# A spectral mixing and gated convolution kernel: blocks in time order, a paired 32x32 convolution, batch 0 turned on chip, single PSUM banks, products shared with GpSimd

## The chip, the cores and the metric

The kernel runs on one core of a Trainium2 chip. Five engines work side by side, each through its own list in order: TensorE (PE, with its weight loads shown as PEld), VectorE (DVE), ScalarE (ACT), GpSimd (POOL) and SyncE (SP, which here only issues DMAs). The time is that of one execution on the device, in microseconds (us). Lower is better.

## What is computed

The input x has 8 batches of 3200 points in time and 256 channels. Along time it is filtered in the frequency domain with one complex filter per channel. The result y then passes a gated unit: a causal convolution of five taps per channel gives the gate, and a gated projection is projected once more.

```python
X = np.fft.rfft(x, axis=1)
Y = X * (filt_r + 1j * filt_i)[None]
y = np.fft.irfft(Y, n=3200, axis=1)
for k in range(5):                       # yp is y with 4 zeros ahead
    gate_pre += conv_w[k][None, None, :] * yp[:, k:k + 3200, :]
gate = 1 / (1 + np.exp(-gate_pre))
out = (gate * (y @ w_val)) @ w_out
```

## The kernel before

Time is written as t = 32 a + r, with a from 0 to 99 (L = 100) and the residue r from 0 to 31 (R = 32). A transform over a, one over r, a product with the filter, and the two inverse transforms make the mixing. In order, for each batch:

- `load_x` (issued by POOL, L161) brings four residues (RC = 4) of all a, converted to bf16, into a tile xt; eight loads a batch, ten buffers.
- `s1` (L417) multiplies by the table cf_t, and `so` copies the result from PSUM to the tile so, of which there is one. `turn` (L436) transposes in 32x32 blocks on DVE into tt, four instructions a batch.
- `s2` (L446) multiplies by w_t in seven units (UCH: six of two frequencies per group and one of one). `xs` copies the unit out of PSUM, `zed` (L464) makes the two products with the real and the imaginary filter on DVE, `inva` (L477) transforms back, `ue` copies to u. The copies `so`, `xs`, `ue` and `oe` are made by one helper, on ACT (L408) or on DVE (L410).
- `wr` (L498, issued by SP) writes u to a DRAM buffer escr, and `lv` (L508, L509) reads it back in another arrangement into vt, four residues at a time in two DMAs, with four buffers. This round trip moves the index from partitions to rows.
- `ib` (L518) multiplies by the table ci_t, `ye` (L528) copies to y on ACT, in the order residue by residue; `halo` (L535, L537) copies the four residues that the causal convolution needs, on POOL.
- For each of eight chunks of four residues, 400 points: `conv` (L545) with 64x64 diagonal matrices, `gate` (L554, sigmoid on ACT), `val` (L563), `gv` (L573, the gate times the value, on DVE), `outp` (L583), `oe`, and `store` in two DMAs (L597, L598).

PSUM is used through four buffers of two banks each (`psum()`). Ahead of the first batch tables are computed, the filters are loaded by POOL in 32 DMAs (L222, L225, L228) and copied to a second group of partitions by SP (L253). Weights come by POOL (`load_w`).

The order on each engine is written by a planner, the class `Plan`: every step is a task with an engine, a booked cost, a rank, its predecessors and the buffers it takes and gives back. The planner runs through the tasks in its own time and picks at each moment the ready task with the lowest rank. What comes out is a fixed list per engine; on the chip an engine works through it in order and waits where a step is not ready. For `s1` the ranks are 8 b + j, and the other stages follow with offsets.

Of the kernel before, what the change touches and what calls it, by code (L numbers as in the profile page):

```python
# [15 lines left out]
PI = math.pi  # L16
L = 100
# [5 lines left out]
NCH = R // RC  # L23
UCH = [(m, min(2, NM - m)) for m in range(0, NM, 2)]
ICH = [NCH - 1] + list(range(NCH - 1))
MAGIC = 12582912.0


class Plan:
# [3 lines left out]
    def __init__(self, room, stay=1.0):  # L33
        self.tasks, self.room, self.stay = {}, dict(room), stay

    def add(self, name, engines, rank, deps, emit, take=(), give=(), land=0.0, mode=None):
        self.tasks[name] = dict(engines=engines, rank=rank, deps=deps, emit=emit, take=take,
                                give=give, land=land, mode=mode)

    def run(self):  # L40
# [6 lines left out]
        ready_at = {n: 0.0 for n in left}  # L47
        free = {}
        mode = None
        gives = []  # L50
        ready = {n for n in left if need[n] == 0}
        order = []
        now = 0.0
        while left:
            gives.sort()
            while gives and gives[0][0] <= now + 1e-9:
                for pool in gives.pop(0)[1]:
                    self.room[pool] += 1
            best = None
            for n in ready:  # L60
                t = left[n]
                if ready_at[n] > now + 1e-9:
                    continue
                if any(self.room[p] < 1 for p in t["take"]):
                    continue
                for e, cost in t["engines"].items():
                    if free.get(e, 0.0) <= now + 1e-9:
                        away = e == "PE" and t["mode"] != mode
                        key = (t["rank"] + (self.stay if away else 0.0), cost)
                        if best is None or key < best[0]:  # L70
                            best = (key, n, e, cost)
            if best is None:
                later = [ready_at[n] for n in ready if ready_at[n] > now + 1e-9]
                later += [v for v in free.values() if v > now + 1e-9]
                later += [g[0] for g in gives if g[0] > now + 1e-9]
                assert later, ("stuck", sorted(ready)[:20], self.room)
                now = min(later)
# [4 lines left out]
            for p in t["take"]:  # L82
                self.room[p] -= 1
            if e == "PE":
# [5 lines left out]
            if t["give"]:  # L90
                gives.append((end + 0.1, t["give"]))
            for u in users.get(n, ()):
                need[u] -= 1
                ready_at[u] = max(ready_at[u], end + 0.1 + t["land"])
                if need[u] == 0:
                    ready.add(u)
            order.append((t["emit"], e))
        self.span = max(free.values())
        return order


@with_exitstack
def kernel(
# [10 lines left out]

# [15 lines left out]
    DQ = D // E  # L130

    cpool = ctx.enter_context(tc.tile_pool(name="const", bufs=1))
    cf_t = cpool.tile([128, 2, 2, 32], FP16, name="cf_t")
    ci_t = cpool.tile([128, L], FP16, name="ci_t")
# [3 lines left out]
    fr_t = cpool.tile([128, 2, NM, D], BF16, name="fr_t")  # L138
    fi_t = cpool.tile([128, 2, NM, D], BF16, name="fi_t")
    dg_t = cpool.tile([128, 2, K, 64], BF16, name="dg_t")  # L140
    wv_t = cpool.tile([128, 2, D], BF16, name="wv_t")
    wo_t = cpool.tile([128, 2, D], BF16, name="wo_t")

    pp = ctx.enter_context(tc.tile_pool(name="ps", bufs=4, space=bass.MemoryType.PSUM))
    dpool = ctx.enter_context(tc.tile_pool(name="scr", bufs=2, space=bass.MemoryType.DRAM))
    NXT = 10
    xpool = ctx.enter_context(tc.tile_pool(name="xin", bufs=NXT))
    sopool = ctx.enter_context(tc.tile_pool(name="s1o", bufs=1))
    tpool = ctx.enter_context(tc.tile_pool(name="s2i", bufs=2))
    zpool = ctx.enter_context(tc.tile_pool(name="zed", bufs=3))  # L150
    upool = ctx.enter_context(tc.tile_pool(name="ivo", bufs=4))

    def psum():
        return pp.tile([128, 1024], FP32, name="ps", tag="ps")

    st = {}

    def load_x(b, j):
        xt = xpool.tile([128, RC, D], BF16, name="xt")
        src = x[b].rearrange("(a r) d -> a r d", r=R)[:, RC * j:RC * j + RC, :]  # L160
        nc.gpsimd.dma_start(out=xt[0:L], in_=src)  # L161
        st["X", b, j] = xt

    g1 = ctx.enter_context(tc.tile_pool(name="gen", bufs=1))
# [10 lines left out]
    V = nc.vector  # L175

# [3 lines left out]
    def frac(t, n, shape):  # L180
        y = g1.tile(shape, FP32, name=f"fy{n}")
        V.tensor_scalar(y[...], t[...], MAGIC, MAGIC, op0=ALU.add, op1=ALU.subtract)
        V.tensor_tensor(y[...], t[...], y[...], op=ALU.subtract)
# [5 lines left out]
    g = {}  # L189

    def fsrc(f, row, ap):
        return bass.AP(tensor=f.tensor, offset=f.offset + row * D, ap=ap)

    FCUT = [(0, 6), (6, NM)]

    def pool_setup():
# [3 lines left out]
        for j in range(3):  # L200
            load_x(0, j)
# [5 lines left out]
        for j in range(3, NCH):  # L207
            load_x(0, j)
# [6 lines left out]
        for m0, m1 in FCUT:  # L215
            nm = m1 - m0
            for f, dst in ((filt_r, fr_t), (filt_i, fi_t)):
                for t in range(2):
                    p = 64 * t
                    k = NM * t + m0  # L220
                    for h in range(2):
                        nc.gpsimd.dma_start(  # L222
                            out=dst[p:p + 16, h, m0:m1, :].rearrange("p m d -> p (m d)"),
                            in_=fsrc(f, k + NS * h, [[100 * D, 16], [1, nm * D]]))
                    nc.gpsimd.dma_start(  # L225
                        out=dst[p + 16:p + 32, 0, m0:m1, :],
                        in_=fsrc(f, 100 - k, [[100 * D, 16], [-D, nm], [1, D]]))
                    nc.gpsimd.dma_start(  # L228
                        out=dst[p + 16:p + 32, 1, m0:m1, :],
                        in_=fsrc(f, 100 - k - NS, [[100 * D, 16], [-D, nm], [1, D]]))  # L230

    def load_w():
        for dh in range(2):
            for r in range(2):
                ch = 128 * dh + 64 * r
                nc.gpsimd.dma_start(
                    out=wv_t[:, dh, :].rearrange("p (r h j) -> p h r j", r=2, h=2)[:, r],
                    in_=moe_w_val[128 * dh:128 * dh + 128, 128 * r:128 * r + 128]
                    .rearrange("p (h j) -> p h j", h=2))
                nc.gpsimd.dma_start(out=wo_t[64 * dh:64 * dh + 64, r, :],  # L240
                                    in_=moe_w_out[ch:ch + 64, :])

    def sp_setup():
        cw = g["cw"] = g1.tile([128, 2, K], FP32, name="cw")
        for dh in range(2):
            nc.sync.dma_start(
                out=cw[:, dh, :],
                in_=moe_conv_w[:, 128 * dh:128 * dh + 128].rearrange("k d -> d k"))
        for m0, m1 in FCUT:
            for dst in (fr_t, fi_t):  # L250
                for t in range(2):
                    p = 64 * t
                    nc.sync.dma_start(out=dst[p + 32:p + 64, :, m0:m1, :],  # L253
                                      in_=dst[p:p + 32, :, m0:m1, :])

    def cf_dve():
# [10 lines left out]
    def cf_act():  # L267
# [3 lines left out]
    def w_dve():  # L271
        pcol = g["pcol"]
        ge = []
        for i, v in enumerate((31.5, 63.5, 95.5)):
# [26 lines left out]
        room = (ypool.tile([128, 2, H + R, L], BF16, name="yt")[...]  # L301
                .rearrange("p h r a -> p (h r a)").bitcast(FP32))
        t, y = (room[:, NS * 64 * n:NS * 64 * n + NS * 64].rearrange("p (s k) -> p s k", k=64)
# [8 lines left out]
    def w_act():  # L312
# [3 lines left out]
    def eye():  # L316
# [9 lines left out]
    TCH = [(0, 4), (4, 8), (8, 12), (12, NM)]  # L326

    def tab_pe(i):
        m0, m1 = TCH[i]
        ps = psum()  # L330
        for m in range(m0, m1):
            for h, t in ((0, 0), (1, 1), (0, 1), (1, 0)):
                rows = slice(64 * h, 64 * h + 64)
                o = 512 * h + 128 * (m - m0)
                nc.tensor.matmul(ps[64 * t:64 * t + 64, o:o + 128],
# [3 lines left out]
        st["tab", i] = ps  # L339

    def tab_ev(i, w, e):
        m0, m1 = TCH[i]
        src = st["tab", i][:, :].rearrange("p (h m b k) -> p h m b k", h=2, b=2, k=64)
# [9 lines left out]
    def ci_dve():  # L353
        vi, vh, vc, vt = col("vi"), col("vh"), col("vc"), col("vt")
        ii = g1.tile([128, 1], I32, name="ii")
        ts(ii[...], g["pcol"][...], 1.0, ALU.mult)
        ij = [g1.tile([128, 1], I32, name=f"ij{n}") for n in range(5)]
        ts(ij[0][...], ii[...], 3, ALU.logical_shift_right)
        ts(ij[4][...], ii[...], 2, ALU.logical_shift_right)
        ts(ij[1][...], ii[...], 1, ALU.logical_shift_right)  # L360
        ts(ij[2][...], ii[...], 1, ALU.bitwise_and)
        ts(ij[3][...], ij[1][...], 1, ALU.bitwise_and)
        ts(ij[1][...], ij[4][...], 1, ALU.bitwise_and)
        for o, n in ((vi, 0), (vt, 1), (vc, 2), (vh, 3)):
# [376 lines left out]
```

## Time and profile before

| What | Value |
|---|---|
| median of 3 runs | 345.65 us (344.83 to 347.17) |
| span of the profiled execution | 344.8 us |
| granted TensorE clock, mean | 0.970 of full |
| instructions in the profile | 9785 |
| hardware DMA queue (SP): packets, MB | 45344, 55.20 |
| software DMA queue (POOL): packets, MB | 12032, 15.08 |

The profile holds one execution. An engine's busy time is the union of its instructions; a matmul's row includes the time that it takes to pass through the array, so a busy PE is not a PE at its peak. A group's row gives line, engine, operation, tiles and shape, the count, then the busy time and the mean of one in ns, then the idle time of the engine ahead of the group and what ended it. In the chain that ended last each piece is followed by what it released; a row has its start, its length and what it is. A row of the stretches has the stretch, its length, the busy time and the instructions of PE, PEld, DVE, ACT and POOL, the granted clock, the mean busy share of the 16 DMA engines and GB/s. The share of the DMA engines counts packets that wait too, and can pass 1.

### The profile page before, as it was taken

What the parts mean: (1) busy time and instruction counts of PE and PEld (TensorE: products, weight loads), DVE (VectorE), ACT (ScalarE), POOL (GpSimd) and SP (SyncE); (2) the same over time, 40 slices, a digit from 0 to 9 for tenths busy, and PEclk for the clock granted to TensorE, in tenths of its full rate; (3) what the DMA queues carried; (4) which work ended last, traced back from release to release, by engine and by line L of the source; (5) the groups of instructions that cost most, each with busy time, mean ns of one, the idle gap of its engine ahead of it and who ended that gap; (6) DMA issues with size and microseconds to landing.
All of it is one profiled execution on the core that took longest, in us unless ns stands there. A gap on an engine that the chain in (4) does not pass through costs nothing.

```text
span 344.8 us, 9785 instructions
## 1 busy us (share of the span) xinstructions
PE 288.3 (84%) x3988; PEld 191.6 (56%) x3988; DVE 256.4 (74%) x340; ACT 267.8 (78%) x309; POOL 68.0 (20%) x142
## 2 busy tenths in 40 slices
PE   2634677639999987999779997999999999999992
PEld 0023031326667755776457764776577677766762
DVE  4985477938698996889849994989798999734541
ACT  3954286928898987898849986998999789887663
POOL 8687455210112112110211011100100000001000
PEclk9999999969999999899989998999999999999997
DMA  6999999995899989898869969795677568778544
GB/s 95 155 168 163 213 192 195 206 238 168 199 232 247 272 233 231 245 229 251 170 200 207 271 176 250 214 245 171 199 208 221 156 204 261 234 214 248 160 144 143
DMA packets 57421, 70.91 MB, mean 206 GB/s; under 512 B 8608, under 2 KB 37152, under 8 KB 57376
## 3 DMA queue, kind: packets, MB, share of 16 engines
q1 hardware_dynamic: 45344, 55.20, 53.4%
q0 software_dynamic: 12032, 15.08, 29.0%
q8 instruction: 31, 0.51, 0.6%
q14 instruction: 14, 0.11, 0.1%
HBM read 43.78 MB, written 39.85 MB: 243 GB/s over the span
## 4 chain that ended last, share of the span: by engine, by line
PE 43%; DMA 24%; DVE 15%; ACT 7%; issue 4%; POOL 4%; SPq 1%; ACTq 0%; POOLq 0%; DVEq 0%
DMA vt<-escr 13%; PE ps L583 12%; PE ps L545 10%; DMA xt<-in_x_dram 6%; PE ps L563 6%; DVE tt L436 5%; DVE gv L573 5%; PE ps L417 5%; PE ps L518 5%; PE ps L477 4%; DMA fi_t<-in_filt_i_dram 3%; PE ps L446 3%; ACT o L408 2%; DVE xs L410 2%; POOL xt L161 2%
## 5 line engine op out<-in xcount | busy, mean ns | idle before, releaser
L573 DVE TENSOR_TENSOR gv<-ps,gt 128x800 bf16<-128x800 f32 x64 | 62.7, 980 | 19.9 <-PE ps L563 13.6
L408 ACT ACTIVATE o<-ps 100x1024 f32<-100x1024 f32 x59 | 61.0, 1035 | 16.9 <-PE ps L583 12.9
L410 DVE CAST xs<-ps 128x1024 bf16<-128x1024 f32 (+1 forms) x44 | 50.4, 1145 | 29.0 <-PE ps L446 29.0
L583 PE MATMUL ps<-wo_t,gv 128*100 128x256 bf16 x512 | 68.7, 278 | 2.7 <-DVE gv L573 1.1
L545 PE MATMUL ps<-yt,dg_t 64*64 64x400 bf16 x1280 | 67.3, 339 | 0.3
L408 ACT ACTIVATE so<-ps 128x1024 bf16<-128x1024 f32 x53 | 54.5, 1029 | 15.9 <-PE ps L417 11.1
L528 ACT ACTIVATE yt<-ps 128x800 bf16<-128x800 f32 x64 | 53.9, 846 | 15.9 <-PE ps L518 15.7
L583 PEld LDWEIGHTS <-gv 128*100 128x100 bf16 x512 | 54.5, 125 | 18.6 <-DVE gv L573 9.0
L161 POOL DMA_DIRECT2D xt<-in_x_dram x64 | 35.4, 556 | 124.5 <-PE ps L417 119.8
L554 ACT ACTIVATE gt<-ps 128x800 bf16<-128x800 f32 x64 | 54.1, 847 | 6.5 <-PE ps L545 5.3
L417 PE MATMUL ps<-xt,cf_t 100*128 100x512 bf16 x128 | 47.5, 462 | 12.2 <-DMA xt<-in_x_dram 11.2
L563 PE MATMUL ps<-yt,wv_t 128*128 128x400 bf16 x256 | 54.4, 335 | 0.5 <-ACT gt L554 0.5
L408 ACT ACTIVATE u<-ps 128x1024 bf16<-128x1024 f32 (+1 forms) x46 | 44.9, 982 | 7.2 <-PE ps L477 6.6
L518 PE MATMUL ps<-ci_t,vt 104*128 104x100 f16 x512 | 34.3, 212 | 16.5 <-DMA vt<-escr 16.4
L518 PEld LDWEIGHTS <-vt 104*128 104x128 bf16 x512 | 29.6, 100 | 30.1 <-DMA vt<-escr 19.8
L545 PEld LDWEIGHTS <-dg_t 64*64 64x64 bf16 x1280 | 34.5, 108 | 17.3 <-issue 4.2
L436 DVE STREAM_TRANSPOSE tt<-so 128x1024 f32<-128x1024 f32 x32 | 40.6, 1272 | 3.2 <-ACT so L408 3.2
L464 DVE TENSOR_TENSOR za<-xs,fr_t 128x1024 bf16<-128x1024 bf16 (+1 forms) x56 | 36.1, 649 | 1.4 <-ACT xs L408 0.2
L464 DVE TENSOR_TENSOR zb<-xs,fi_t 128x1024 bf16<-128x1024 bf16 (+1 forms) x56 | 35.5, 640 | 1.4 <-DMA fi_t<-in_filt_i_dram 1.4
L477 PE MATMUL ps<-zb,b_t 64*64 64x256 bf16 x416 | 29.7, 294 | 4.4 <-DVE zb L464 4.4
L477 PE MATMUL ps<-za,a_t 64*64 64x256 bf16 x416 | 30.3, 298 | 2.4 <-DVE za L464 2.1
L446 PE MATMUL ps<-tt,w_t 64*64 64x256 bf16 x416 | 24.2, 305 | 9.0 <-DVE tt L436 4.4
(93 smaller groups left out, 181.9 us busy)
## 6 DMA issues: line engine op xcount, KB each, us to landing
out_dram<-o SPq DMA_DIRECT2D x64, 384.0 KB
xt<-in_x_dram POOLq DMA_DIRECT2D x64, 200.0 KB, 6.7
escr<-u SPq DMA_DIRECT2D x48, 256.0 KB
vt<-escr SPq DMA_DIRECT2D x64, 192.0 KB
escr<-u SPq DMA_DIRECT2D x8, 128.0 KB
vt<-escr SPq DMA_DIRECT2D x64, 16.0 KB
out_dram<-o SPq DMA_DIRECT2D x64, 16.0 KB
fr_t<-in_filt_r_dram POOLq DMA_DIRECT2D x8, 56.0 KB, 4.7
```

Of the source, the lines that this page charges most:

```text
L408: nc.scalar.activation(dst, src, AF.Copy, **kw)
L410: nc.vector.tensor_copy(dst, src)
L417: nc.tensor.matmul(ps[:, 512 * h:512 * h + 512], lhsT=cf_t[0:L].rearrange("p h c i -> p (h c i)"), rhs=xv[:, DQ // 2 * h:DQ // 2 * h + DQ ...
L436: nc.vector.transpose(dst, src)
L464: (nc.vector if e == "DVE" else nc.gpsimd).tensor_tensor(z[:, :, 0:nm * D], xs_[:, :, 0:nm * D], f[:, :, m0:m0 + nm, :].rearrange("p h m d ...
L477: nc.tensor.matmul(ps[64 * h:64 * h + 64, 512 * t + D * a:512 * t + D * a + D], lhsT=tab[rows, h, m0 + a, :], rhs=zz[w][rows, h, D * a:D * ...
L518: nc.tensor.matmul(ps[:, o:o + L], lhsT=v[0:NV, a, 128 * dh:128 * dh + 128], rhs=ci_t[0:NV, :], start=True, stop=True)
L545: nc.tensor.matmul(ps[64 * dh:64 * dh + 64, 512 * r:512 * r + RC * L], lhsT=dg_t[rows, dh, k, :], rhs=y[rows, dh, RC * j + k:RC * j + k + ...
L554: nc.scalar.activation(g[...], ps[:, :].rearrange("p (h n) -> p h n", h=2)[:, :, 0:RC * L], AF.Sigmoid)
L563: nc.tensor.matmul(ps[:, 512 * eh:512 * eh + RC * L], lhsT=wv_t[:, dh, 128 * eh:128 * eh + 128], rhs=y[:, dh, H + RC * j:H + RC * j + RC, ...
L573: nc.vector.tensor_tensor(gv_[...], ps[:, :].rearrange("p (h n) -> p h n", h=2)[:, :, 0:RC * L], g[...], op=ALU.mult)
L583: nc.tensor.matmul(ps[0:L, D * a:D * a + D], lhsT=gv_[:, eh, L * a:L * a + L], rhs=wo_t[:, eh, :], start=(eh == 0), stop=(eh == 1))
```

## The change

The kernel is rewritten around the same mathematics.

- y is stored in time order: `ye` writes runs of four points. The halo copy is gone. The gated unit works on blocks of 512 points, six and one of 128 (`BLOCKS`). `conv` takes two blocks at a time (`PAIRS`), with sixteen 32x32 tiles in place of four 64x64 ones; it depends on all `ye` of its batch. `outp` reads every fourth point of a block as its stationary operand, 128 rows at a time instead of 100, and `store` writes four rows of 1 KB per partition in one DMA.
- Batch 0 doesn't go through DRAM: `ue` writes to a tile of its own layout, and `turn2`, four DVE transposes, makes vt out of it; `ib` and `ye` of batch 0 run per half of the channels, with a second column of the table ci_t.
- PSUM is one tile of eight banks. The planner hands out single banks; `val`, `gv`, `outp` and `oe` work on one bank each, in halves.
- In batches 1 to 7 the products of units 0, 2, 3, 5 and 6 are made by GpSimd (`pool_u`), those of 1 and 4 by DVE. The list books 0.15 + 1.05 nm us for one of them, 2.25 us for a full unit (nm = 2).
- x is loaded by eight residues (XR = 8), four loads a batch, six buffers. `turn` works in place, in two so tiles. vt is one tile of a whole batch, with one DMA for four residues. The filters come in 24 DMAs. `ci_dve` moves from DVE to POOL, `diag` from DVE to ACT.
- The planner has a model of the DMA queues and of the banks, and each stage and batch has a rank of its own, written in a table (`CFG`).

```diff
+XR = 8
+NXC = R // XR
-ICH = [NCH - 1] + list(range(NCH - 1))
+BLK = 512
+BLOCKS = [(i * BLK, BLK) for i in range(6)] + [(6 * BLK, 128)]
+PAIRS = [(0, 1), (2, 3), (4, 5), (6,)]
+CFG = dict(
+    turned=(0,),
+    pool_u=((), (0, 2, 3, 5, 6)),
+    room=dict(xt=6, so=2, xs=3, z=4, u=4, e=2, v=8, y=2, g=4, gv=4, o=3),
...
+            if u in cfg["pool_u"][min(b, 1)]:
+                for w in range(2):
+                    add(f"z{b},{u},{w}", {"POOL": 0.15 + 1.05 * nm}, "z", b, u,
...
+                add(f"z{b},{u}", {"DVE": 0.06 + 0.545 * nm}, "z", b, u, [f"xs{b},{u}"] + fl,
...
+            for q in range(4):
+                add(f"t2{b},{q}", {"DVE": 1.16}, "t2", b, q, [f"ue{b},{u}" for u in range(NU)]
...
+            add(f"cv{b},{p}", {"PE": 1.12 if len(js) == 2 else 0.35}, "cv", b, js[0], yes + ["dg"],
+                ("conv", b, p), banks=2 * len(js), take=("g",) * len(js), mode=2)
...
+    PS = pp.tile([128, NB, 512], FP32, name="ps")
+    VT = vpool.tile([128, R, D], BF16, name="vt")
...
+    def load_x(e, b, c):
+        xt = xpool.tile([128, XR, D], BF16, name="xt")
+        src = x[b].rearrange("(a r) d -> a r d", r=R)[:, XR * c:XR * c + XR, :]
         nc.gpsimd.dma_start(out=xt[0:L], in_=src)
...
+    def turn(e, b, q):
+        v = words(st["SO", b], q)
+        nc.vector.transpose(v, v)
...
+    def turn2(e, b, q):
+        w = D // 8
+        ut = st["UT", b][...].bitcast(FP32)
+        src = bass.AP(tensor=ut.tensor, offset=ut.offset + NS * w * q,
+                      ap=[list(ut.ap[0]), [2 * NS, DQ // 4], [1, 2], [2, 32]])
+        dst = (VT[...].rearrange("p r d -> p (r d)").bitcast(FP32)
+               .rearrange("p (r n) -> p n r", r=R)[:, w * q:w * q + w]
+               .rearrange("p (q w) r -> p q w r", w=2))
+        nc.vector.transpose(dst, src)
...
-        nc.sync.dma_start(out=v[0:96], in_=sv[0:96])
-        nc.sync.dma_start(out=v[96:NV], in_=sv[96:NV])
+        nc.sync.dma_start(out=VT[0:NV, RC * i:RC * i + RC, :], in_=sv)
...
+        y = st["Y", b][:, hs[0]:hs[-1] + 1, H:]
+        nc.scalar.activation(
+            y.rearrange("p h (a r) -> p h a r", r=R)[:, :, :, RC * i:RC * i + RC],
+            st.pop(("ib", b, i, hs))[:, :, 0:RC * L].rearrange("p h (r a) -> p h a r", r=RC),
+            AF.Copy, scale=1.0 / N)
+
+    def conv(e, b, p, bk):
+        y = st["Y", b]
+        js = PAIRS[p]
+        tiles = [(i, j) for s in range(4) for i in range(4) for j in [(i + s) % 4]]
+        for k in range(K):
+            for i, j in tiles:
+                ih, half = divmod(i, 2)
+                dh, x = j & 1, ih ^ (j >> 1)
+                if x >= len(js):
+                    continue
+                n0, n = BLOCKS[js[x]]
+                rows = slice(32 * i, 32 * i + 32)
+                nc.tensor.matmul(PS[32 * j:32 * j + 32, bk[2 * x + half], 0:n],
+                                 lhsT=dg_t[rows, dh, k, :], rhs=y[rows, dh, n0 + k:n0 + k + n],
+                                 start=(k == 0), stop=(k == K - 1))
...
+            for a in range(2):
+                for r in range(2):
+                    nc.tensor.matmul(PS[:, bk[0], D * a:D * a + D],
+                                     lhsT=gv_[:, r, 2 * h + a:n:4], rhs=wo_t[:, j & 1, r, :],
+                                     start=(r == 0), stop=(r == 1))
...
+            nc.sync.dma_start(out=out[b, n0:n0 + n].rearrange("(p i) d -> p (i d)", i=4),
+                              in_=o[...].rearrange("p h n -> p (h n)"))
```

More of the change, by code (lines that the diff above doesn't have):

```diff
@@ L89, in run @@
             free[e] = end
[L90 to L97, printed above, removed]
+            self.start[n] = (now, end, e)
+            freed = [] if t["free"] is None else [held[k][i] for k, ii in t["free"] for i in ii]
```

892 lines of the change are left out of this document (503 added, 389 removed), and 33 rows, old and new, of the table move.

## The prediction

> **What bounds the kernel now.** I read the page's busy line and its slices, then stretches by stage, then the chain that ended last, then the groups kept apart by shape.
>
> ```profile
> span 344.8 us, 9785 instructions
> ...
> PE 288.3 (84%) x3988; PEld 191.6 (56%) x3988; DVE 256.4 (74%) x340; ACT 267.8 (78%) x309; POOL 68.0 (20%) x142
> ...
> PE   2634677639999987999779997999999999999992
> ...
> DVE  4985477938698996889849994989798999734541
> ACT  3954286928898987898849986998999789887663
> ...
> DMA  6999999995899989898869969795677568778544
> ...
> DMA packets 57421, 70.91 MB, mean 206 GB/s; under 512 B 8608, under 2 KB 37152, under 8 KB 57376
> ...
> PE 43%; DMA 24%; DVE 15%; ACT 7%; issue 4%; POOL 4%; SPq 1%; ACTq 0%; POOLq 0%; DVEq 0%
> ```
>
> No engine is the bound alone. Three are near full in the middle (the digits 8 and 9), GpSimd is idle for 80% of the span, and the first nine slices (78 us) are thin on PE, DVE and ACT while the DMA row is full. So there are two stories: a slow start, and a middle in which three engines and the DMA hand work to each other. The chain shows both.
>
> ```profile
> 26.16 5.19 DMA fi_t<-in_filt_i_dram
> 34.36 11.60 DMA xt<-in_x_dram
> ...
> 63.07 11.63 DMA vt<-escr
> 74.75 0.85 PE ps L518 x8
> ...
> 154.53 1.25 DVE tt L436
> ...
> 193.72 1.25 DVE tt L436
> ...
> 231.22 1.25 DVE tt L436
> ...
> 265.55 1.25 DVE tt L436
> ...
> 302.11 0.97 PE ps L545 x20
> 303.08 1.01 PE ps L583 x8
> 304.08 0.68 PE ps L563 x4
> ```
>
> The turn (L436) recurs once a batch: 39.2, 37.5 and 34.3 us apart. At the start the chain goes filters, the next batch's input, the read back of batch 0 from DRAM. I cut the span at the convolution (L545) of the first and of the last batch.
>
> ```profile
> 79.12 1.89 PE L545 MATMUL ps<-yt,dg_t 64*64 64x400 bf16 x40
> ...
> 315.01 2.09 PE L545 MATMUL ps<-yt,dg_t 64*64 64x400 bf16 x40
> ```
>
> That gives 79.1 us of start, 235.9 us for seven batch steps (33.7 each), and 29.8 us from 315.0 to 344.8.
>
> **The evacuations, the turn and the products (DVE and ACT).** These are the groups that change.
>
> ```profile
> L408 ACT ACTIVATE o<-ps 100x1024 f32<-100x1024 f32 x59 | 61.0, 1035 | 16.9 <-PE ps L583 12.9 <-ACT yt L528 1.5 <-DMA vt<-escr 1.4
> ...
> L528 ACT ACTIVATE yt<-ps 128x800 bf16<-128x800 f32 x64 | 53.9, 846 | 15.9 <-PE ps L518 15.7
> ...
> L408 ACT ACTIVATE u<-ps 128x1024 bf16<-128x1024 f32 x40 | 41.4, 1040 | 5.8 <-PE ps L477 5.1 <-ACT xs L408 0.4 <-DMA vt<-escr 0.2
> L436 DVE STREAM_TRANSPOSE tt<-so 128x1024 f32<-128x1024 f32 x32 | 40.6, 1272 | 3.2 <-ACT so L408 3.2
> L161 POOL DMA_DIRECT2D xt<-in_x_dram x64 | 35.4, 556 | 124.5 <-PE ps L417 119.8 <-DMA xt<-in_x_dram 2.1 <-DMA fi_t<-in_filt_i_dram 0.9
> ...
> L464 DVE TENSOR_TENSOR za<-xs,fr_t 128x1024 bf16<-128x1024 bf16 x48 | 32.8, 689 | 1.2
> L464 DVE TENSOR_TENSOR zb<-xs,fi_t 128x1024 bf16<-128x1024 bf16 x48 | 32.5, 682 | 1.4 <-DMA fi_t<-in_filt_i_dram 1.4
> ...
> L410 DVE COPY o<-ps 100x1024 f32<-100x1024 f32 x5 | 6.1, 1222 | 4.7 <-PE ps L583 3.4 <-DMA vt<-escr 1.4
> ...
> L408 ACT ACTIVATE u<-ps 128x512 bf16<-128x512 f32 x6 | 3.6, 593 | 1.5 <-PE ps L477 1.5
> ...
> L464 DVE TENSOR_TENSOR za<-xs,fr_t 128x512 bf16<-128x512 bf16 x8 | 3.2, 405 | 0.2 <-ACT xs L408 0.2
> L464 DVE TENSOR_TENSOR zb<-xs,fi_t 128x512 bf16<-128x512 bf16 x8 | 3.1, 390 | 0.0
> ```
>
> Products: in batches 1 to 7, four full units and the half unit go to GpSimd, 4 x (0.689 + 0.682) + 0.405 + 0.390 = 6.28 us a batch, 44.0 us off DVE. Output copies: 64 of 1024 columns become per batch twelve of 512 and one of 256, 6400 columns for 8192, so 0.22 x (61.0 + 6.1) = 14.7 us go; there are 104 of them, 40 more, and the u rows put the fixed part of one at 2 x 593 - 1040 = 146 ns, so 5.8 us come back. The gated products (L573) become 104 for 64 in the same way, 5.8 us more; the gates fall from 64 to 56, 1.2 us less. Batch 0 adds four turns, 5.1 us, and eight more y copies, 1.2 us. Sum: -44.0 - 14.7 + 5.8 + 5.8 - 1.2 + 5.1 + 1.2 = -42.0 of 524.2 us (256.4 + 267.8), 8%. The lists balance the two engines, so I apply it to both: 30.1 us a batch each for 32.8.
>
> The y copy writes runs of four points and reads PSUM with a stride of 100. No row has that. I take 0, since the equal 1024-column copies above cost the same whatever they write (1035 and 1040). The upper end is a doubling, 0.85 x 8 = 6.8 us a batch on ACT; a lower price than contiguous has no reason.
>
> **PE.** By the chain, twenty convolution matmuls take 0.97 us, eight output ones 1.01, four value ones 0.68. Output falls from 64 to 50 matmuls a batch: 14 x 0.126 = 1.8 us less. Its stationary operand is now read with a stride of four; I take 0, and the other end is that the loads stop hiding behind the matmuls, one more 0.126 for each of the 50, 6.3 us. The convolution does five taps with sixteen 32x32 tiles at a time on 512 points each, a pair of blocks at once. If sixteen tiles overlap as the four 64x64 tiles do, a pair costs 0.97 x 512/400 = 1.24 us and the last 128 points at most 0.97 x 128/400 = 0.31: 4.0 us a batch for 7.8. If only four overlap, it costs 16 us. I take the first, because x20 in 0.97 us (49 ns each, for 400 columns) already shows tiles running together. [...] PE loses 5.6 us a batch of 36.0 (288.3 / 8), value and the other stages being the same columns. New here: a convolution waits for all eight y copies of its batch, not for two. Behind it in PE's order stand the value and output matmuls; the cover is the next batch's first stages, placed between, and two y buffers.
>
> **GpSimd, and what waits behind it.** A product there has no row; the halo copies are nearest.
>
> ```profile
> L537 POOL COPY yt<-yt x16: 511/515/653, 76.5 to 313.1; 128x396 bf16<-128x396 bf16 x16
> ```
>
> ```profile
> 283.21 0.68 DVE L464 TENSOR_TENSOR zb<-xs,fi_t 128x1024 bf16<-128x1024 bf16 x1
> ...
> 283.61 1.11 POOL L537 COPY yt<-yt 128x396 bf16<-128x396 bf16 x2 [27.73 <-ACT yt L528]
> ```
>
> One input of 396 elements takes 0.515 us, 1.3 ns each; a product of 1024 is between 1.33 us (the second input free) and 2.66 (each input read for itself). The new list books 2.25, which I use: 8 x 2.25 + 2 x 1.2 = 20.4 us a batch, and four loads of 0.556 make 22.6, under a 30 us step at either end. The input loads now stand in POOL's queue behind products, up to 4.5 us late; six buffers of a quarter batch each cover that.
>
> The longest copy, 0.653 us, is in the pair that starts at 283.61, inside a DVE product that ends at 283.89. It is the only sign of a collision: up to 0.14 us for 0.28 us of overlap. The other way round, a DVE product behind a GpSimd product, no row shows. Four products a batch stay on DVE, between those of GpSimd; each may wait from 0 to 2.25 us, 0 to 9 us a batch. I take 0.5 each, 2 us, between the row and the ends. [...]
>
> **The start.** SP's queue is part of it.
>
> ```profile
> 34.22 28.63 SPq L498 DMA_DIRECT2D escr<-u  x8
> ```
>
> Reading batch 0 back could not begin before 63.07, because SP's order puts a write of batch 1 ahead, and it lasted 11.63 us. Both go. In their place come four turns (5.1 us) and y copies (8 x 0.846 + 1.2 = 8.0 us, beginning after two turns). The filters set the earliest point: the last lands at 31.35; they now take 24 issues for 32, some 4 us less of POOL's queue at 0.556, so 27, and 4 us for the copy to the other partitions, then 3 us for the last unit: 34. Then 2.5 + 8 = 44.5, and batch 1's first stage uses the same engines: 50 us, with 44 and 60 as ends (60: the input of batch 1 again blocks PE, as the 11.60 us piece does). Constants moved to GpSimd and ACT lie inside these 50 us; I cost them at nothing, and if GpSimd is late with the table of L518, the y copies wait.
>
> **The steps.** Stores and reads back are one DMA each instead of two, so SP has about half the issues; SP was not the bound.
>
> ```profile
> 0.00:50.00 50.00, 26.39 (x220) 10.10 (x221) 33.28 (x85) 28.38 (x33) 33.64 (x72) 1.00 0.97 162
> ...
> 110.00:260.00 150.00, 137.05 (x1995) 96.60 (x1994) 124.74 (x144) 128.57 (x150) 17.86 (x37) 0.97 0.85 222
> ```
>
> From 110 to 260 us PE is busy 91%, ACT 86%, DVE 83%. A step of 33.7 less 8% is 31.0. The waits for DRAM on the chain in the steps (5 to 7 us a batch where they stand) shrink, since a whole batch of read-back slots stands free instead of half and single PSUM banks let copies free space sooner: I take 2.5 us off, and add the 2 us of collisions: 30.5. The end loses PE work, 1.8 + 3.8 = 5.6 us: 24.2.
>
> Sum: 50 + 7 x 30.5 + 24.2 = 287.7 us of span, against 344.8. The median of the runs, 345.65, is 0.9 above that span, so 289 us by the clock of the runs.
>
> **Rivals.** (1) DVE waits for GpSimd at half a product each time, 1.13 x 4 = 4.5 us a batch instead of 2: 33 us a step, 306. For it: the one overlap above; against: DVE has slack of 17%. (2) The DMA binds. Batch 0's trip (104 x 32 x 256 x 2 bytes each way, 3.4 MB) goes, 67.5 MB stay; 8.1 MB move in the first 50 us, so 59.4 MB in 238 us is 250 GB/s, where 110 to 260 shows 222 at a share of 0.85. If 222 is the limit, the rest takes 268 us: 319. Against: 0.85 is not full; 222 / 0.85 = 261. (3) The tiles overlap less than said: eight at once make the convolution cost 8 us a batch as now, PE keeps 36.0 - 1.8 = 34.2 us a step and becomes the bound, and the end is 28: 318. (4) Faster still: the lists are packed without gaps. Then copies overlap at their ends, as these two do.
>
> ```profile
> 202.59 1.02 ACT L408 ACTIVATE so<-ps 128x1024 bf16<-128x1024 f32 x1 [0.78 <-ACT gt L554]
> 203.51 1.02 ACT L408 ACTIVATE o<-ps 100x1024 f32<-100x1024 f32 x1
> ```
>
> They start 0.92 us apart and last 1.02, so 30.1 us of copies fit into 27 to 28; with a start of 45 and steps of 27.5 that is 263. Against: PE has 30 us of its own by the same kind of sum.
>
> (5) Slower: GpSimd becomes the bound. It has 9 product sizes and 2.2 us of loads a batch; to lose, a step must reach 38.6 us ((345.65 - 0.9 - 50 - 24.2) / 7), so a product must take (38.6 - 2.2) / 9 = 4.0 us. At twice the booked time, 4.5 us, a step is 42.7 and the kernel 374. Against: the rows' upper end is 2.66, and DVE holding it off adds at most 0.69.
>
> **Chances.** Forecast 0.57 (its own range 274 to 304), rivals in order 0.14, 0.09, 0.05, 0.09, 0.06. A measurement here tells about 1% from no change. Faster by more: the forecast and rivals 1 to 4, 0.94, of which I give 0.02 to within 1%, where two of them come together; slower: 0.06. Leaving out rival 5, the upper half of 2 and the lower part of 4 gives 266 to 317.
>
> **What would show it.** The first convolution near 50 us; turns some 30 us apart; L545's successor at 1.2 to 1.6 us a pair; GpSimd busy for 20 to 24 us a batch, with no idle ended by PE; DVE products still near 0.68. DVE products over 1.5 us show rival 1; a DMA row of nines with engines waiting for vt, rival 2; pairs over 2.4 us, rival 3; products of 4 us on GpSimd, rival 5. I am wrong if the first convolution is after 60 us or the steps exceed 34.

## The result and the profile after

The changed kernel takes 464.95 us (median of four runs, 459.59 to 471.43) where the kernel before took 345.72 beside it: 1.336 times as long, 95% interval 1.327 to 1.346. Ratios leave out executions in a slower state of the chip, such as the 471.43 here, while medians count all. The forecast was 289. From here on line numbers are those of the changed kernel (`so`, `xs`, `ue`, `oe` copy in L428 on ACT and L430 on DVE; `s1` L702, `s2` L730, products L750 on DVE and L753 on POOL, `inva` L763, `turn2` L793, `ib` L816, `ye` L827, `conv` L844, `gate` L853, `val` L860, `gv` L870, `outp` L880). The experiments with neighbouring banks have eight lines more ahead of them, so 8 is added to each.

The page after, in the same order as before:

```profile
span 463.1 us, 11221 instructions
...
PE 306.0 (66%) x4804; PEld 175.9 (38%) x4804; DVE 274.3 (59%) x343; ACT 247.1 (53%) x315; POOL 192.8 (42%) x214
...
PE   3533677677556576665875679755686697768794
...
DVE  5862969768753654674474548654447664326464
ACT  4824766556264536563564548743366374536553
POOL 6688549374435615554310460555127650000000
PEclk9995755689795679996796989975579698879999
DMA  7991982454462166726596134661244248355244
...
DMA packets 47689, 67.57 MB, mean 146 GB/s; under 512 B 5208, under 2 KB 31704, under 8 KB 47640
...
PE 39%; ACT 22%; DVE 19%; issue 5%; DMA 4%; SPq 0%; ACTq 0%; DVEq 0%
```

Apart from GpSimd (192.8 us for 68.0), no engine does much more than before, and none is near full any more: the digits of PE, DVE and ACT are mostly 4 to 7 in the middle, where they were mostly 8 and 9, and the DMA row is at half. Rows of fives on all engines at once suggest engines that wait for each other. The stretches from the first convolution to the last say the same, before and then after:

```profile
79.00:315.00 236.00, 220.87 (x3261) 157.00 (x3257) 192.14 (x221) 203.92 (x237) 24.42 (x51) 0.98 0.82 219
```

```profile
76.00:440.00 364.00, 249.95 (x4079) 144.77 (x4080) 209.75 (x243) 191.96 (x236) 139.50 (x90) 0.81 0.48 144
```

DVE and ACT together are busy 401.7 us where it was 396.1, in 364 us instead of 236. The start is 3 us shorter and the end 6; seven steps of 33.7 us became seven of 52.0. All of the loss is in the steps. On DVE and ACT it is idle time; PE is busy 29 us longer, at a granted clock of 0.81 instead of 0.98. What single instructions cost is near the forecast (groups by shape):

```profile
L753 POOL TENSOR_TENSOR z<-xs,f_t 128x1024 bf16<-128x1024 bf16 x56 | 122.1, 2196 | 115.8 <-ACT xs L428 76.7 <-DVE xs L430 36.4 <-PE ps L763 2.6
...
L750 DVE TENSOR_TENSOR z<-xs,f_t 128x1024 bf16<-128x1024 bf16 x40 | 49.0, 1266 | 11.6 <-ACT xs L428 6.4 <-DMA f_t<-f_t 5.0
...
L827 ACT ACTIVATE yt<-ps 128x800 bf16<-128x800 f32 x56 | 46.9, 837 | 47.1 <-PE ps L816 11.5 <-DVE so L430 9.2 <-DVE xs L430 6.7
L844 PE MATMUL ps<-yt,dg_t 32*32 32x512 bf16 x1920 | 44.3, 469 | 9.5 <-ACT yt L827 3.9 <-ACT so L428 1.4 <-ACT u L428 1.3
L428 ACT ACTIVATE so<-ps 128x1024 bf16<-128x1024 f32 x41 | 41.2, 1023 | 27.5 <-PE ps L702 14.5 <-PE ps L763 2.9 <-DVE xs L430 2.5
```

GpSimd's product takes 2.20 us (2.25 booked), the y copy 0.84, a PSUM copy 1.02 as before. The odd thing stands at the right, in what ended the idle time: a y copy that waits for `so` on DVE, `conv` that waits for `so` and `u` on ACT. These steps share no data. PE may have to wait until a copy gives back a bank, but a copy on ACT and one on DVE need nothing of each other. The list of waits is full of such pairs (engine, line, what it waited for; us in all, times, the longest):

```profile
DVE o L430 <- ACT gt L853: 10.4, 3, 4.0
...
ACT yt L827 <- DVE so L430: 9.2, 6, 2.1
...
DVE so L430 <- ACT yt L827: 7.6, 4, 2.7
...
ACT yt L827 <- DVE xs L430: 6.7, 3, 3.0
```

And in the timeline one sees it happen:

```profile
94.82 1.23 DVE L430 CAST so<-ps 128x1024 bf16<-128x1024 f32 x1 [0.70 <-PE ps L880]
96.08 0.60 ACT L428 ACTIVATE o<-ps 128x512 f32<-128x512 f32 x1 [1.61 <-DVE so L430]
96.57 1.02 ACT L428 ACTIVATE so<-ps 128x1024 bf16<-128x1024 f32 x1
...
96.73 0.30 PE L763 MATMUL ps<-z,a_t 64*64 64x256 bf16 x4 [1.23 <-ACT o L428]
...
97.62 1.23 DVE L430 CAST xs<-ps 128x1024 bf16<-128x1024 f32 x1 [1.58 <-ACT so L428]
...
98.90 0.71 PE L860 MATMUL ps<-yt,wv_t 128*128 128x512 bf16 x2 [1.00 <-DVE xs L430]
```

DVE copies until 96.05, only then ACT starts; ACT copies until 97.59, only then DVE starts; then PE. Three engines take turns over PSUM, each on its own banks: in the planner's list DVE's `so` at 94.82 reads banks 4 and 7, ACT's `o` bank 5 and its `so` banks 1 and 2, DVE's `xs` at 97.62 banks 0 and 3, and the matmuls of L860 at 98.90 write bank 1.

### The profile page after: what moved, and what is told of

Read it like the earlier page. It is cut to its first block, busy times and chain, and to the rows that moved or that the text cites. A ratio compares the mean times of both kernels' runs of the same rounds, so it can differ in the third digit from the quotient of the medians.

```text
span 463.1 us, 11221 instructions
## 1 busy us (share of the span) xinstructions
PE 306.0 (66%) x4804; PEld 175.9 (38%) x4804; DVE 274.3 (59%) x343; ACT 247.1 (53%) x315; POOL 192.8 (42%) x214
## 2 busy tenths in 40 slices
DMA packets 47689, 67.57 MB, mean 146 GB/s; under 512 B 5208, under 2 KB 31704, under 8 KB 47640
## 4 chain that ended last, share of the span: by engine, by line
PE 39%; ACT 22%; DVE 19%; issue 5%; DMA 4%; SPq 0%; ACTq 0%; DVEq 0%
PE ps L844 9%; ACT yt L827 8%; PE ps L880 7%; PE ps L860 6%; PE ps L816 5%; PE ps L763 5%; DVE z L750 5%; PE ps L702 5%; DVE so L430 4%; ACT gt L853 4%; ACT so L428 3%; ACT xs L428 3%; ACT u L428 3%; DVE u L430 3%; DVE xs L430 3%
## 5 line engine op out<-in xcount | busy, mean ns | idle before, releaser
L753 POOL TENSOR_TENSOR z<-xs,f_t 128x1024 bf16<-128x1024 bf16 (+1 forms) x70 | 137.9, 1988 | 148.8 <-ACT xs L428 106.4
L870 DVE TENSOR_TENSOR gv<-ps,gt 128x512 bf16<-128x512 f32 (+1 forms) x112 | 67.9, 628 | 58.8 <-ACT gt L853 18.2
L827 ACT ACTIVATE yt<-ps 128x800 bf16<-128x800 f32 (+1 forms) x72 | 53.7, 766 | 47.1 <-PE ps L816 11.5
L853 ACT ACTIVATE gt<-ps 128x1024 bf16<-128x1024 f32 (+1 forms) x56 | 50.6, 931 | 52.3 <-PE ps L844 21.8
L860 PE MATMUL ps<-yt,wv_t 128*128 128x512 bf16 (+1 forms) x224 | 66.4, 404 | 17.2 <-ACT gt L853 7.0
L880 PE MATMUL ps<-wo_t,gv 128*128 128x256 bf16 x384 | 57.8, 280 | 12.9 <-ACT u L428 4.6
L702 PE MATMUL ps<-xt,cf_t 100*128 100x512 bf16 x128 | 52.0, 506 | 17.5 <-DMA xt<-in_x_dram 9.4
L816 PE MATMUL ps<-ci_t,vt 104*128 104x100 f16 (+1 forms) x512 | 40.8, 235 | 31.7 <-ACT yt L827 15.7
L844 PE MATMUL ps<-yt,dg_t 32*32 32x512 bf16 (+1 forms) x2240 | 49.4, 439 | 12.6 <-ACT u L428 4.5
L750 DVE TENSOR_TENSOR z<-xs,f_t 128x1024 bf16<-128x1024 bf16 (+1 forms) x42 | 49.7, 1226 | 11.7 <-ACT xs L428 6.4
L428 ACT ACTIVATE so<-ps 128x1024 bf16<-128x1024 f32 x41 | 41.2, 1023 | 27.5 <-PE ps L702 14.5
L816 PEld LDWEIGHTS <-vt 104*128 104x128 bf16 (+1 forms) x512 | 34.8, 113 | 49.2 <-issue 40.1
L430 DVE COPY o<-ps 128x512 f32<-128x512 f32 (+1 forms) x49 | 32.5, 669 | 33.7 <-ACT gt L853 10.4
L880 PEld LDWEIGHTS <-gv 128*128 128x128 bf16 x384 | 39.9, 116 | 29.9 <-issue 20.1
L730 PE MATMUL ps<-so,w_t 64*64 64x256 bf16 x416 | 29.0, 338 | 33.2 <-ACT yt L428 10.6
L763 PE MATMUL ps<-z,a_t 64*64 64x256 bf16 x416 | 33.9, 327 | 18.9 <-ACT yt L827 7.7
L428 ACT ACTIVATE xs<-ps 128x1024 bf16<-128x1024 f32 (+1 forms) x32 | 30.5, 956 | 23.4 <-PE ps L763 5.9
L430 DVE CAST so<-ps 128x1024 bf16<-128x1024 f32 x23 | 27.9, 1221 | 25.0 <-ACT yt L827 7.6
L428 ACT ACTIVATE u<-ps 128x1024 bf16<-128x1024 f32 (+1 forms) x32 | 31.5, 984 | 20.7 <-DMA escr<-u 3.1
L428 ACT ACTIVATE o<-ps 128x512 f32<-128x512 f32 (+1 forms) x55 | 30.9, 578 | 21.2 <-PE ps L880 12.1
L844 PEld LDWEIGHTS <-dg_t 32*32 32x32 bf16 x2240 | 29.8, 93 | 31.4 <-issue 25.8
```

What stands on the lines that cost most here:

```text
L428: nc.scalar.activation(dst, src, AF.Copy, **kw)
L430: nc.vector.tensor_copy(dst, src)
L702: nc.tensor.matmul(PS[:, bk[h], :], lhsT=cf_t[0:L].rearrange("p h c i -> p (h c i)"), rhs=xv[:, DQ // 2 * h:DQ // 2 * h + DQ // 2], start= ...
L750: nc.vector.tensor_tensor(z[:, k, :, 0:nm * D], xs_[:, :, 0:nm * D], f[:, k], op=ALU.mult)
L753: (nc.vector if e == "DVE" else nc.gpsimd).tensor_tensor(z[:, w, :, 0:nm * D], xs_[:, :, 0:nm * D], f[:, w], op=ALU.mult)
L816: nc.tensor.matmul(PS[:, bk[n], L * a:L * a + L], lhsT=VT[0:k, RC * i + a, 128 * dh:128 * dh + 128], rhs=ci_t[0:k, int(b in turned), :], s ...
```

## The experiments

**Theory A.** PSUM is one tile now, and the planner hands out any two free banks. A step on two banks reaches them as one access with a stride, `PS[:, bk[0]:bk[1] + 1:bk[1] - bk[0], :]`. If the program's waits are placed by the range from the first bank to the second, a copy of banks 1 and 6 is put in order with everything on banks 2 to 5, though it touches none of them. The rivals B and C are readings in which it plays no part where the banks lie.

**Neighbouring banks.** The planner gives a two-bank step an aligned pair.

```diff
+        def pick(k):
+            if k > 1:
+                done = [v for v in range(0, NB, 2) if v in banks and v + 1 in banks]
...
-                mine = held[n] = sorted(banks[:t["banks"]])
-                del banks[:t["banks"]]
+                mine = held[n] = pick(t["banks"])
```

> The planner hands out PSUM banks in aligned neighbouring pairs (0,1), (2,3), (4,5), (6,7) instead of any two free ones; nothing else is edited, but the list shifts a little since a pair must be free. Theory A (false order: two instructions that share no bank wait for each other because the address range from the first to the second bank of one encloses a bank of the other): the waits of ACT for DVE and of DVE for ACT between copies vanish, 285 to 315 us. Theory B (GpSimd and DVE exclude each other, which makes products late and the rest with them): nothing changes, 445 to 470 us. Theory C (the list itself is out of step with the chip): 430 to 470 us.

**The same banks and the same list, each two-bank copy as two of one bank.**

```diff
-        copy(e, xs_[:, :, 0:nm * D], st.pop(("s2", b, u))[:, :, 0:nm * D])
+        ps = st.pop(("s2", b, u))
+        for h in range(2):
+            copy(e, xs_[:, h, 0:nm * D], ps[:, h, 0:nm * D])
```

(`so`, `ue`, `ye` and the gate are split likewise.)

> List and banks as in the changed kernel, but each copy of two banks is made by two instructions of one bank each, so no instruction spans banks that it does not use. It adds some 290 instructions on ACT and DVE at about 0.1 us, 15 us on each engine. Theory A: 320 to 350 us. Theories B and C: 465 to 485 us.

Neighbouring banks: 362.57 us, 1.054 of before (1.020 to 1.088). Split copies: 361.26 in one run, although it has 11638 instructions. Both pages:

```profile
span 360.5 us, 11233 instructions
...
PE 272.7 (76%) x4804; PEld 170.5 (47%) x4804; DVE 281.0 (78%) x340; ACT 244.3 (68%) x318; POOL 193.3 (54%) x214
```

```profile
span 359.6 us, 11638 instructions
...
PE 277.6 (77%) x4804; PEld 164.7 (46%) x4804; DVE 285.8 (79%) x408; ACT 252.0 (70%) x538; POOL 193.4 (54%) x214
```

The second keeps every bank and the order of the list, and takes the stride out of the accesses by halving the copies. It gains 104 us, the neighbouring banks 102 without any halves. So the loss isn't the banks' own speed (a two-bank `so` on ACT took 1.02 us in the changed kernel and with neighbouring banks) but the order that the strided access forces. B, with 445 us or more, and C, with 430 or more, fall. A's size was too hopeful: some 73 us above the forecast remain.

The list of waits says the same. The waits of ACT for DVE and of DVE for ACT sum to 9.5 us before, 158.8 in the changed kernel, 16.3 with neighbouring banks and 18.1 with split copies. The largest two with neighbouring banks are of steps that share data (`gv` uses the gate, `z` uses `xs`):

```profile
DVE gv L878 <- ACT gt L861: 7.6, 4, 3.9
...
DVE z L758 <- ACT xs L436: 4.6, 1, 4.6
```

In the changed kernel there are 54 waits of 0.2 us or more, 85.4 us in all, in which ACT or DVE starts a step on PSUM (y copies not counted) within 0.1 us of the end of the other's and takes no data from it. By the planner's list none of the 54 pairs shares a bank, and in 52 of them, 84.7 us, the ranges from first to last bank overlap. The trace shows these waits as semaphores; where in the making of the program they are set, no run here shows.

**The same in the kernel before.** Its four PSUM buffers become pairs of one tile, once banks k and k + 4, once neighbours. In both the buffers are used strictly in turn, so that some copies read another step's values.

```diff
-    pp = ctx.enter_context(tc.tile_pool(name="ps", bufs=4, space=bass.MemoryType.PSUM))
+    pp = ctx.enter_context(tc.tile_pool(name="ps", bufs=1, space=bass.MemoryType.PSUM))
+    PS = pp.tile([128, 8, 512], FP32, name="ps")
...
+        return PS[:, FIRST[k]:FIRST[k] + STEP + 1:STEP, :]
```

> The kernel before with the same list, but PSUM as one tile of eight banks, and its four buffers are the banks (0,4), (1,5), (2,6), (3,7), whose ranges all overlap. Theory A: PE, ACT and DVE take turns on PSUM, 430 us or more. Theories B and C: no change, 343 to 348 us, since no product is on GpSimd and the list is the old one.

> Control for the last one: the kernel before with PSUM as one tile of eight banks and the buffers (0,1), (2,3), (4,5), (6,7). All theories: 343 to 349 us.

838.58 us with the far pairs, 349.27 with the near ones, one run each. With k and k + 4 all four ranges overlap, and the kernel runs almost one step at a time: DVE and ACT are busy 31 and 34%. The waits between ACT and DVE sum to 276.9 us against 7.6. Of the three theories only A has a difference here, and it is a factor of 2.4 between two kernels that differ in a start and a stride.

**With no product on GpSimd, banks as in the change.** The waits might have been GpSimd's, handed on from engine to engine. Here the list is made with `pool_u=((), ())`, and the constants of `ci_dve` are on DVE.

> The changed kernel with its banks as they are (any two free banks), the table and all products on VectorE: GpSimd makes no product. It tells whether the order forced by the ranges of banks acts by itself. Theory A (it does): nothing of it goes away with GpSimd's work; against 330.6 with neighbouring banks the time is 400 to 450. Rival G (the waits that went with neighbouring banks were mostly waits for GpSimd's late products, handed on from engine to engine): with no product on GpSimd the time is 330 to 350 with any banks.

442.36 us, 1.284 of before (1.267 to 1.302). G falls: the order by ranges acts without GpSimd.

**What is left at 362.** In the run with neighbouring banks the products on DVE stand out, and the start does.

```profile
187.01 8.35 POOL L761 TENSOR_TENSOR z<-xs,f_t 128x1024 bf16<-128x1024 bf16 x4
...
189.19 7.33 DVE L758 TENSOR_TENSOR z<-xs,f_t 128x1024 bf16<-128x1024 bf16 x2
...
195.97 0.43 PE L771 MATMUL ps<-z,a_t 64*64 64x256 bf16 x4 [5.27 <-DVE z L758]
```

GpSimd has four products on end until 195.36. DVE's two begin at 189.19 and last 7.33 us together, and the inverse matmuls that need the first of them start at 195.97, 0.6 us behind GpSimd's last: the first DVE product, at 6.73 us the longest of this run, stood until GpSimd was through. PE waited 5.27 us. The other wait is that of ACT for the table's constants on GpSimd:

```profile
ACT sx L470 <- POOL fyx L466: 10.1, 1, 10.1
```

Four kernels on these (the list is made anew in each):

```diff
-    fixed("cid", {"POOL": 4.5}, sr["ci"], ["s1"], ("ci_dve",))
+    fixed("cid", {"DVE": 4.5}, sr["ci"], ["s1"], ("ci_dve",))
...
-            G.tensor_scalar(o, i, s, 0.5 * s - 0.5, op0=ALU.mult, op1=ALU.add)
+            V.tensor_scalar(o, i, s, 0.5 * s - 0.5, op0=ALU.mult, op1=ALU.add)
```

> The run with neighbouring banks, and one thing more: the constants of the table that the y copies' stage uses are computed on VectorE again, not on GpSimd. Theory T (the late table is what holds up the start): the 10.1 us that ScalarE waited for GpSimd before sx go, the first convolution stands near 64 us instead of 74, and the time is 347 to 355. Rival S (the start's own turns and filters set it; the table only happened to be last): the first convolution stays at 70 us or later and the time within 1% of 362.

then beside that `pool_u=((), (0, 1, 2, 3, 4, 5, 6))`, `pool_u=((), ())`, or `turned=()`:

> As the run with the table on VectorE, and all seven units' products of batches 1 to 7 are on GpSimd, so that VectorE has no product to run beside one of GpSimd's. Theory D (VectorE's products wait for whole GpSimd products, some 1.35 us each, 37 us in all, and most of it lies on the path): GpSimd gets 13 products of 2.2 us and 2.2 us of loads a batch, 31 us, still below a step; steps fall from 37 to about 34 us and the time is 320 to 335. Rival F (the waits of VectorE were slack, and the order of the list holds the steps): GpSimd at 31 us a batch is late for the inverse stage and the time is 345 to 370, not below the run with the table on VectorE.

> As the run with the table on VectorE, and no product is on GpSimd. Theory D: a VectorE product takes 0.69 us again; VectorE gets 6.3 us of work a batch back and loses 5.3 us of waits, so the time is within 3% of the run with the table on VectorE, 335 to 355, and GpSimd's products bring nothing. Rival F (the waits were slack): VectorE is the fuller engine and every us of it shows: 6.3 us a batch, 370 to 395.

> As the run with the table on VectorE, and batch 0 goes through DRAM like the others, as it did before the change. Theory T: turning batch 0 on chip is worth what the forecast gave it once the table is in time; without it the first convolution moves from near 64 to 80 us and the time rises by 10 to 16 us. Rival S: the four turns, at 1.9 us each, and the copies behind them are what sets the start, and the time stays within 1.5% of the run with the table on VectorE.

| Kernel (neighbouring banks in all) | us | ratio to before, 95% | first conv | step | end | DVE product, ns |
|---|---|---|---|---|---|---|
| nothing more | 362.57 | 1.054 (1.020 to 1.088) | 73.6 | 37.7 | 23.2 | 1611 |
| table on DVE | 335.45 | 0.962 (0.954 to 0.970) | 69.2 | 34.3 | 21.6 | 1248 |
| and all products on GpSimd | 390.99 | 1.122 (1.115 to 1.130) | 66.5 | 42.9 | 22.0 | 682 |
| and all products on DVE | 330.61 | 0.946 (0.938 to 0.954) | 87.7 | 31.3 | 22.0 | 679 |
| and batch 0 by DRAM | 359.47 | two runs, 354.86 and 364.08 | 95.9 | 33.7 | 21.3 | 1220 |

(First conv, step and end are cut at the convolutions as in the prediction; in the last kernel one eighth of batch 5's positions is taken from batch 6.) The table on DVE brought 27 us, more than T had expected, and only 4.4 of it at the start. Batch 0 by DRAM is later by 26.7 us at the first convolution and by 19 and 29 us in its two runs, where T had 10 to 16 (the numbers that order its list were not made for it). With no product on DVE beside GpSimd's, a product takes 0.68 us on DVE, as before the change, and 1.22 to 1.61 in the three kernels of the table where some are beside them; so much of D holds. The two bounds of D's time didn't hold: all products on DVE cost no more than sharing them, 330.6 against 335.5, below D's 335 to 355, and all on GpSimd gave 391, above both theories. GpSimd's queue shows one likely reason:

```profile
131.61 12.53 POOL L761 TENSOR_TENSOR z<-xs,f_t 128x1024 bf16<-128x1024 bf16 x6 [2.61 <-DVE xs L438]
...
144.14 6.28 POOL L761 TENSOR_TENSOR z<-xs,f_t 128x1024 bf16<-128x1024 bf16 x3
152.04 4.35 POOL L761 TENSOR_TENSOR z<-xs,f_t 128x512 bf16<-128x512 bf16 x3 [1.63 <-DVE xs L438]
156.33 3.31 POOL L443 DMA_DIRECT2D xt<-in_x_dram  x6
```

The loads of x stand behind 23 us of products, and then six are issued at once. In this run PE waited 18.8 us for GpSimd's products and 8.1 us for x; what each cost was not separated.

**The same list.** In those kernels the order changed with the engine. Two more change the engine that executes and leave the order: the table's constants on DVE in the list of the first row, and GpSimd's products on DVE in the list of the second.

```diff
-            (nc.vector if e == "DVE" else nc.gpsimd).tensor_tensor(
+            nc.vector.tensor_tensor(
```

> The run with neighbouring banks (362.6 us), with the order of its list untouched: the table's constants are computed on VectorE at the place where the list has them on GpSimd. The earlier run with the table on VectorE also had its list made anew, and its gain of 27 us lay mostly in the steps. Theory T (the late table alone): the 10.1 us of waiting for sx go, the first convolution moves from 74 to about 64 us, the steps stay at 37 to 38 us, and the time is 350 to 356. Rival L (the new order of the list brought most of it): the time stays above 356. Rival E (early work late shifts everything behind it): 333 to 342, as with the new list.

> The run with neighbouring banks and the table on VectorE (335.5 us), with the order of its list untouched: the products that GpSimd made are made by VectorE at the same places. VectorE gains 7 x 6.3 = 44 us of work and loses some 21 us of waiting for GpSimd, 23 us more of 331. Theory D (the order is the same and only the exclusion goes): about half of that shows, 340 to 352. Rival W (a wait for GpSimd costs more than itself, since copies behind it in VectorE's order come late for PE): the time falls or stays, 325 to 337.

The table: 360.06 us, 1.038 (1.032 to 1.045). The first convolution came at 66.8 instead of 73.6, and the steps took 38.4: what the start gained was given back. Rival L holds: the other 25 us came with the new order. The products: 339.91 us, 0.984 (0.977 to 0.991), beside 0.962 with sharing; a touch below D's range. The DVE products of the four lists:

```profile
L758 DVE TENSOR_TENSOR z<-xs,f_t 128x1024 bf16<-128x1024 bf16 x40 | 64.2, 1650 | 0.3
```

```profile
L758 DVE TENSOR_TENSOR z<-xs,f_t 128x1024 bf16<-128x1024 bf16 x40 | 48.1, 1248 | 1.9 <-DMA f_t<-f_t 1.8
```

```profile
L758 DVE TENSOR_TENSOR z<-xs,f_t 128x1024 bf16<-128x1024 bf16 x40 | 25.4, 681 | 1.4 <-DMA f_t<-f_t 1.4
```

```profile
L758 DVE TENSOR_TENSOR z<-xs,f_t 128x1024 bf16<-128x1024 bf16 x96 | 60.1, 679 | 5.2 <-ACT xs L436 2.7 <-DMA f_t<-f_t 2.5
```

(Table in the old list; table in the new list; that list with the products on DVE; all products on DVE in a list of its own.) Of 40 products 28 can meet GpSimd's. In the old list they wait 37.0 us over 40 x 0.68, in the new one 20.9. So an order that lets fewer products meet goes with a time 25 us shorter; whether the meetings are all that this order mends isn't settled. Moving 44 us of work to GpSimd in one and the same list brings 2.2% of before by the two ratios, 8 us (4.5 us by the two medians).

**The list searched again** for all products on DVE: only the numbers of `CFG` that order it, and the price of `turn2`, differ.

> The run with neighbouring banks, the table and all products on VectorE, with nothing changed but the numbers from which the list is ordered: they were searched again for this split of the work, with the turn of batch 0 priced at its measured 1.92 us; the list's own plan falls from 290.9 to 283.8 us and its first convolution from 75.9 to 59.2 us. Theory L (what is left above the forecast is mostly the order of the list, late first convolution above all): 315 to 325. Rival N (the list's plan isn't what holds the time now; the handovers that it doesn't price are): within 1% of 330.6.

Four runs gave 321.5, 322.7, 331.9 and 332.0, in two groups 3% apart, so no ratio is stated and the time decides neither for L nor for N. The first convolution of the profiled execution (span 319.8) is at 66.8 instead of 87.7, and steps are 33.1 instead of 31.3: a 21 us earlier start gave 9 us.

## Why the prediction was wrong

**The step that failed** is in the sum of the steps: "single PSUM banks let copies free space sooner", counted with the waits for DRAM as 2.5 us off a step. The price of reaching two banks that don't lie side by side was never asked. In its place came some 14 us on each step (52.0 against 37.7 with neighbouring banks, seven times 14.3 = 100 of the 102 us that they bring). None of the rivals held it: all five were about engines and transfers, none about the order among the accesses. The only one that made the kernel slower, rival 5, asked for products of 4.0 us on GpSimd, and they took 2.20. The line to stop at was in the changed kernel, `two(bk)`, which takes two banks as one strided access.

**GpSimd beside DVE.** I took 0.5 us of waiting for a DVE product. In the changed kernel it was (49.0 - 40 x 0.68) / 28 = 0.78 us, in the run with neighbouring banks (62.8 - 27.2) / 28 = 1.27: rival 1's size, 1.13, once the engines are close. The row of before on which I leaned showed a GpSimd copy up to 0.14 us late beside a DVE product; the two DVE products above took 7.33 us beside GpSimd's, for 2 x 0.68. GpSimd's own product loses little in the mean: 2.13 us in the run with all products on it, 2.18 to 2.23 where DVE has some.

**The start.** Forecast 50 us, measured 75.9, and "I am wrong if the first convolution is after 60 us". "Constants moved to GpSimd and ACT ... I cost them at nothing": ACT waited 10.6 us for the table, and with neighbouring banks 6.8 us of such a wait (10.1 us) reached the first convolution in the same list. The rest lies in three other steps; how much each adds, no run separates. I let only "the last unit" follow the filters, but in the run with all products on DVE all seven inverse units lie between 31 and 46 us. The four turns, 1.92 us each where I took 1.27, don't stand together (the same run):

```profile
48.19 1.94 DVE L801 STREAM_TRANSPOSE vt<-yt 128x1024 f32<-128x1024 f32 x1
...
49.95 1.24 DVE L729 STREAM_TRANSPOSE so<-so 128x1024 f32<-128x1024 f32 x1
51.08 1.91 DVE L801 STREAM_TRANSPOSE vt<-yt 128x1024 f32<-128x1024 f32 x1
...
52.81 1.23 DVE L729 STREAM_TRANSPOSE so<-so 128x1024 f32<-128x1024 f32 x1
...
55.12 1.92 DVE L801 STREAM_TRANSPOSE vt<-yt 128x1024 f32<-128x1024 f32 x1 [1.08 <-PE ps L824]
...
59.57 1.92 DVE L801 STREAM_TRANSPOSE vt<-yt 128x1024 f32<-128x1024 f32 x1 [1.48 <-PE ps L824]
```

The list puts batch 1's turns (L729) between batch 0's (L801), and the last two wait for PE. And the sixteen y copies of batch 0, which I put at 8 us, run from 56.1 to 77.5 us in the changed kernel, with gaps. My 50 us knew that batch 1 uses the same engines and priced that at 5.5.

**What held.** The bytes: 67.57 MB for 67.5. The end: 23.5 us for 24.2. GpSimd's product: 2.20 for 2.25. The y copy with its short runs: 0.84 for 0.846, so the doubling at the upper end was empty. DVE and ACT: 270.2 + 253.9 = 524.1 us with all products on DVE; less the 44.0 us of them that the forecast had on GpSimd, 480.1, where 524.2 - 42.0 = 482.2 was forecast. The tiles overlap: 24 pairs take 44.3 us after, 1.85 us each, and 37.0 us, 1.54 each, in the run with all products on DVE, under rival 3's 2.4 but above my 1.24; the shortest pairs of the changed kernel took 1.35. The 1.6 us that ended my range for a pair is worked out from no row and no run here; the two means are what was measured in its place. These terms move the time by a few us a batch; the sum was right about the work and silent on its order.

With the order by ranges gone the kernel is still 5% longer than before; with the table on DVE and the list made anew it is 4% shorter, with all products on DVE too 5%. What remains from 330.6 to 289 is the start, 38 us (87.7 for 50), and the steps, 6 us (31.3 for 30.5 each), less 2 us at the end. In the list searched again, at 321.5, the start and the steps have 17 and 18 us of it.

## What to carry to other kernels

Before costing an edit that splits a buffer, look at how the pieces are addressed: an access that strides over memory it doesn't touch may be ordered against everything in between (halving the copies brought 104 of 465 us here). When all engines show fives, read what ends the idle time and ask of each pair whether one needs the other; a pair that shares no data may be a wait the program made, and splitting the access in two with all else kept tells in one run. Work given to GpSimd is priced with what it holds up on VectorE (a mean of 1.61 us for a product of 0.68 with neighbouring banks) and with the loads behind it in its queue (six behind 23 us of products), not by its own duration.

## What the runs showed of the hardware

In these runs the granted clock was lower where PE was busy for less of the span: 0.97 before with PE at 84%, 0.95 with all products on DVE at 80%, 0.89 with neighbouring banks at 76%, 0.81 in the changed kernel at 66%; with the far pairs it was 0.645. PE's busy time is itself longer at a lower clock: in the changed kernel a convolution pair took 1.35 us where the granted clock was 1.00 (at 89.24, 261.68 and 375.68 us) and 2.36 us where it was 0.50 (at 253.35 and 334.45). Its mean of 1.85 us, against 1.54 with all products on DVE, makes it seem that waits are paid twice; no run here held the clock fixed. A DVE product can stand through several of GpSimd's: with neighbouring banks one took 6.73 us beside three of them, ten times its own 0.68, while two others, from 131.48 us on, took 2.54 and 2.61 us, 1.9 beyond their own time where one of GpSimd's lasts 2.13. And the transposes of the same 128x1024 words took 1.92 us in `turn2` and 1.24 in `turn`, both with all products on DVE. The two differ in how they stride through their tiles; whether that is the cause, no run here shows.
